# Weights ahead of the second chunk, attention behind the first group, squares shared between two engines

## The chip, the cores and the metric

The kernel runs on one core of a Trainium2 chip. The metric is the device time of one execution in microseconds (us). The core has a matrix engine (PE, with its weight loads shown as PEld), a vector engine (DVE), a scalar engine (ACT), a general engine (POOL), which also issues most of the loads, and SP, which issues the stores and some transposes. Each engine runs its own instructions in the order in which the program writes them and waits on semaphores for the others.

## The reference

Two layers, one behind the other. The first is a decaying linear attention over 4 batches, 8 heads, 768 positions and a head width of 64:

```python
for b in range(nb):                       # 12 blocks of 64 positions
    intra = einsum('bhic,bhjc->bhij', qb, kb) * Dmask      # lam ** (i - j), lower triangle
    intra = einsum('bhij,bhjd->bhid', intra, vb)
    inter = einsum('bhid,bhde->bhie', qb * lam_pow, kv_state)
    out[:, :, sl] = intra + inter
    kv_state = lam_block * kv_state + einsum('bhsd,bhse->bhde', kb * rev_pow, vb)
```

Its output, seen as 3072 rows of 512, goes through a two-layer network with 2048 hidden columns:

```python
h = x @ w_in
s = sin(alpha * h)
g = h + s * s / alpha
return g @ w_out
```

## The kernel before

The 768 positions are cut into six chunks of 128. One chunk of all four batches is a group of 512 rows; the network runs group by group (g = 0 to 5). For a group there are 16 hidden blocks of 128 columns (f = 0 to 15). `hidden(g, f)` issues four PE matmuls into a PSUM bank (L386), a sine on ACT (L389) and, for most f, the square on ACT too (L392). `finish(g, f)` issues on DVE the square, where `squarer` gives it to DVE (L400), and then the sum that writes one block of `gall` and frees the bank (L401). Three banks turn in rotation, so that `hidden(g, f)` needs the bank that `finish(g, f - 3)` frees; in group 0 the first seven blocks have a bank each.

The second matrix product is cut into 16 **units** a group: unit (m, part) is four matmuls (L411), which add four `gall` blocks times a quarter of `w_out` into the bank of 128 output rows m. The fourth part of an m is followed by `store(g, m)`: a copy out of PSUM, on ACT for group 0 and on DVE for groups 1 to 3, and a store issued by SP. Units wait in a list, `behind`; `run(n)` issues the next n of them. For group 0 the list has the parts of m = 0 and 1 in turn, then those of m = 2 and of m = 3.

The attention of chunk t = g + 1 has to be written into `xt[g + 1]` before `hidden(g + 1, 0)` can start. Chunks 0 and 1 are done whole, one batch b at a time: `turns` (eight PE transposes of k and q and one copy to SBUF on ACT, L235), `scores1` (eight matmuls, L256, and two DVE products with the decay mask, L260) and `outs` (four matmuls with the state, L267, eight with v, L271, and one DVE product that writes `xt`, L278). `states1` makes the state after a chunk (L286 on PE, L294 or L297 on DVE, casts on POOL, L301). From chunk 2 on the steps stand in slots of the group's loop: states and `update` (L315, L297), `scores` and `masks` (L334, L341), `outputs` and `leave` (L352, L360, L368), and `turn_by_dma` transposes k and q by DMA. `decay_k` is a POOL product (L204) that the states need.

The program's order is written out by hand. Group 0's loop holds the attention of batch 0 and part of batch 1 of chunk 1 in its last three turns, and four units, at f = 10, 12, 14 and 15. Between group 0 and group 1 stands the **bridge**: the rest of chunk 1's attention with three units between. Group 1's loop calls `run(1)` in every turn but 0, 2, 4, 6, 10 and 12, which takes the nine units that are left. From group 2 on each turn has one unit of the group before.

POOL issues the loads in order: chunk 0, `w_in` in five transfers, `w_out` 0 and 1, `decay_k` of chunk 0 and the six loads of chunk 1 in mixed order, `w_out` 2 and 3, then the loads of chunk 2. Half a chunk is two batches (called "a" and "b" below); each of k, q and v is one transfer a half.

Of the kernel before, what the change touches and what calls it, by code (L numbers as in the profile page):

```python
# [11 lines left out]
BF16 = mybir.dt.bfloat16  # L12
# [3 lines left out]
def kernel(  # L16
# [11 lines left out]
    nc = tc.nc  # L28
# [5 lines left out]
    HP = H // 2  # L34
# [23 lines left out]
    def bank(nm, n, dtype=FP32):  # L58
        return psum.tile([P, 512 if dtype is FP32 else 1024], dtype, name=nm, tag=f"b{n}")
# [28 lines left out]
    def load_w_in(i):  # L88
        nc.gpsimd.dma_start(out=w_in_sb[i][:],
                            in_=moe_w_in[:, i * 512:(i + 1) * 512].rearrange("(c p) g -> p c g", p=P))  # L90

    def load_w_in0(n):
        w = slice(256 * n, 256 * n + 256)
        nc.gpsimd.dma_start(out=w_in_sb[0][:, :, w], in_=moe_w_in[:, w].rearrange("(c p) g -> p c g", p=P))

    def load_w_out(i):
        nc.gpsimd.dma_start(out=w_out_sb[i][:],
                            in_=moe_w_out[i * 512:(i + 1) * 512, :].rearrange("(f p) d -> p f d", p=P))

    def load(t, nm, b0, b1):  # L100
        dst, src = NAT[nm]
        nc.gpsimd.dma_start(  # L102
            out=dst[t][:, b0:b1, :, :].rearrange("p b h e -> p (b h) e"),
            in_=src[b0:b1, :, t * T:(t + 1) * T, :].rearrange("b h p e -> p (b h) e"))
# [13 lines left out]
    iden = consts.tile([P, P], BF16, name="iden")  # L118
# [19 lines left out]
        load(0, nm, b0, b1)  # L138
    load_w_in0(0)
    load_w_in0(1)  # L140
    for i in range(1, 4):
        load_w_in(i)

    lnlam = consts.tile([P, H], FP32, name="lnlam")
    nc.scalar.activation(out=lnlam[:], in_=lam_bc[:], func=ACTF.Ln)
# [40 lines left out]
    V, G, A = nc.vector, nc.gpsimd, nc.scalar  # L186
    xt = {}
    kdec = {}
    KT, QT, both = {}, {}, {}
    STm = {}  # L190
    def home(t, blk):
        return SBD[2 if blk else t % 2]

    def new_xt(t):
        xt[t] = xtp.tile([P, NDC, GRP], BF16, name="xt")
# [4 lines left out]
    def decay_k(t, b0, b1):  # L200
        if t not in kdec:
            kdec[t] = kdp.tile([P, B, H, D], BF16, name="kdec")
        R = later["R128" if t < 2 else "R64"]
        nc.gpsimd.tensor_tensor(out=kdec[t][:, b0:b1, :, :], in0=kn[t][:, b0:b1, :, :],  # L204
                                in1=R[:].unsqueeze(1).unsqueeze(3).broadcast_to([P, b1 - b0, H, D]),
                                op=ALU.mult)

    def new_turned(t):
        QKT = trp.tile([P, 2, B, HP, T], BF16, name="QKT")
        KT[t], QT[t] = QKT[:, 0], QKT[:, 1]  # L210
        both[t] = QKT
# [9 lines left out]
    def turns(t, b, n, engines=None):  # L221
        ps = bank("T_ps", n, BF16)[:].rearrange("p (n c i) -> p n c i", n=2, c=HP)
        if t not in KT:
            new_turned(t)
        for n, src in enumerate((kn, qn)):
            for hp in range(HP):
                nc.tensor.transpose(out=ps[:, n, hp, :], in_=src[t][:, b, 2 * hp:2 * hp + 2, :], identity=iden[:])  # L227
        if engines:
            for n, eng in enumerate(engines):
                if eng is nc.scalar:  # L230
                    eng.copy(out=both[t][:, n, b, :, :], in_=ps[:, n])
                else:
                    eng.tensor_copy(out=both[t][:, n, b, :, :], in_=ps[:, n])
        else:
            nc.scalar.copy(out=both[t][:, :, b, :, :], in_=ps)  # L235

    def halves(hd):
        return slice(hd * D, (hd + 1) * D)

    def turns_pair(t, nm, b, bk, engines):  # L240
        ps = bank("T_ps", bk, BF16)[:].rearrange("p (u c i) -> p u c i", u=2, c=HP)
        src, n = (kn, 0) if nm == "k" else (qn, 1)
        for u in range(2):
            for hp in range(HP):
                nc.tensor.transpose(out=ps[:, u, hp, :], in_=src[t][:, b + u, 2 * hp:2 * hp + 2, :], identity=iden[:])
        for u, eng in enumerate(engines):
            if eng is nc.scalar:
                eng.copy(out=both[t][:, n, b + u, :, :], in_=ps[:, u])  # L248
            else:
                eng.tensor_copy(out=both[t][:, n, b + u, :, :], in_=ps[:, u])  # L250

    def scores1(t, b, ns):
        Fb = [bank("F0_ps", n)[:].rearrange("p (c i) -> p c i", c=HP) for n in ns]
        for hp in range(HP):
            for hd in range(2):
                nc.tensor.matmul(out=Fb[hd][:, hp, :], lhsT=KT[t][halves(hd), b, hp, :],  # L256
                                 rhs=QT[t][halves(hd), b, hp, :], start=True, stop=True)
        st = work.tile([P, 2, HP, T], BF16, name="STm")
        for hd in range(2):
            nc.vector.tensor_tensor(out=st[:, hd], in0=Fb[hd], in1=C0[:, hd], op=ALU.mult)  # L260
        STm[t, b] = st

    def outs(t, b, n, eng=None):
        O = bank("O_ps", n)[:].rearrange("p (c i) -> p c i", c=HP)
        if t:
            for hp in range(HP):
                nc.tensor.matmul(out=O[:, hp, :], lhsT=home(t, 0)[:, b, hp, :, :], rhs=QT[t][:, b, hp, :],  # L267
                                 start=(hp == 0), stop=False, skip_group_check=True)
        for hp in range(HP):
            for hd in range(2):  # L270
                nc.tensor.matmul(out=O[halves(hd), hp, :], lhsT=vn[t][:, b, 2 * hp + hd, :],  # L271
                                 rhs=STm[t, b][:, hd, hp, :], start=(t == 0 and hp == 0), stop=True,
                                 skip_group_check=True)
        x = xt[t][:, :, b * T:(b + 1) * T]
        if eng is nc.scalar:
            nc.scalar.copy(out=x, in_=O)
        else:
            nc.vector.tensor_tensor(out=x, in0=O, in1=Etab[:], op=ALU.mult)  # L278
# [95 lines left out]

    def squarer(g, f):
        if g == 0:
            return V if f in (1, 4, 7, 10, 13) else A
        if g == 1:
            return V if f in (2, 5, 8, 11) else A
        return A  # L380
# [56 lines left out]
    def spin(n, cols=512):  # L437
        ps = bank("hps", HB[0])
        for _ in range(n):
            nc.tensor.matmul(out=ps[:, 0:cols], lhsT=fill[:, 0:P], rhs=fill[:, 0:cols], start=True, stop=True)  # L440
# [20 lines left out]
    nc.tensor.transpose(out=a_ps[:, 0:NFC], in_=alpha_fp[:], identity=idf[:])  # L461
    alpha_sb = consts.tile([P, NFC], FP32, name="alpha_sb")
    r_sb = consts.tile([P, NFC], FP32, name="r_sb")
    turns_pair(0, "k", 2, 1, (A, A))
    spin(6)
    turns_pair(0, "q", 2, 2, (A, V))
    nc.vector.tensor_copy(out=alpha_sb[:], in_=a_ps[:, 0:NFC])
    nc.vector.reciprocal(out=r_sb[:], in_=alpha_sb[:])
    scores1(0, 2, (6, 7))
# [5 lines left out]
    outs(0, 2, 1)  # L475
    outs(0, 3, 2)
    spin(2)
    load_w_out(0)
    load_w_out(1)
    decay_k(0, 0, 2)  # L480
    load(1, "k", 0, 2)
    load(1, "q", 0, 2)
    decay_k(0, 2, 4)
    load(1, "v", 0, 2)
    for nm in "kqv":
        load(1, nm, 2, 4)
    load_w_out(2)
    load_w_out(3)


    new_xt(1)
# [19 lines left out]
    def run(n):  # L511
        for _ in range(min(n, len(behind))):
            behind.pop(0)()

    queue_units(0, [(m, part) for part in range(4) for m in (0, 1)] + [(m, part) for m in (2, 3) for part in range(4)])
    for f in range(NFC):
        hidden(0, f)
        if f in (6, 9):
            states1(0, f // 3 - 2, 4 + 2 * (f == 9))
        if f == 13:  # L520
            turns(1, 0, 6)
        if f == 14:
            scores1(1, 0, (4, 5))
            turns(1, 1, 6)
        if f in (10, 12, 14):
            run(1)
        if f == 15:
            scores1(1, 1, (4, 5))
            outs(1, 0, 6)
            run(1)  # L530
        finish(0, f)
    pair_load(2, 0)
    pair_load(2, 1)
    mask_table()

    outs(1, 1, 1)
    turns(1, 2, 2)
    turns(1, 3, 6)
    run(1)
    scores1(1, 2, (4, 5))  # L540
    run(1)
    scores1(1, 3, (0, 1))
    outs(1, 2, 2)
    outs(1, 3, 6)
    run(1)
    decay_k(1, 0, 2)
    decay_k(1, 2, 4)
    pair_ready(2, 0)
# [35 lines left out]
    for g in range(1, NT + 1):  # L584
        if g < NT:
            gall[g] = gbp.tile([P, NFC, GRP], BF16, name="gall")
        at = slots(g) if g + 1 < NT else {}
        fd = feed(g) if g + 1 < NT else {}
        if g + 1 < NT:
            new_xt(g + 1)  # L590
        for i in range(NFC):
            if g == NT and not behind:
                break
            for a in fd.get(i, []):
                a[0](*a[1:])
            if g < NT:
                hidden(g, i)
            for a in at.get(i, []):
                a[0](*a[1:])
            if g > 1 or i not in (0, 2, 4, 6, 10, 12):  # L600
                run(1)
            if g < NT:
                finish(g, i)
        if g < NT:
            queue_units(g, [(m, part) for m in range(B - 1 if g == NT - 1 else B) for part in range(4)])
# [31 lines left out]
```

## Time and profile before

| what | value |
|---|---|
| median of 3 runs | 215.86 us (215.69 to 217.07) |
| the profiled execution's own time | 215.78 us |
| its span, from first to last instruction | 214.1 us |
| PE busy / DVE busy / ACT busy / POOL busy | 200.0 / 139.0 / 140.6 / 96.4 us |
| group 0's first hidden matmul | 20.40 us |
| group 1's first hidden matmul | 49.67 us |
| end of the attention that group 2 needs | 76.34 us |

The 1.7 us between the span and the time lie around the instructions. PE is busy for 93% of the span, but busy time of PE holds the stretched times of matmuls whose inputs are late, so it is read beside the order of the instructions and not alone. Matmul rows of one merged line follow each other; the distance from one start to the next is the time that a step takes, which is less than the duration of a single record.

### The profile page before, as it was taken

To read this page: it belongs to the slowest core of one execution; us is meant where nothing else is said; L and a number is where in the kernel's file an instruction comes from. 1 tells how busy PE (TensorE), PEld (TensorE's weight loads), DVE (VectorE), ACT (ScalarE), POOL (GpSimd) and SP (SyncE) were. 2 spreads that over 40 slices of the span, in tenths; PEclk is the share of its full clock that TensorE was granted. 3 is DMA by queue.
4 is the path that set the end of the run, shared out by engine and by line. 5 is a ranking of instruction groups with operands and counts; after the bars stand their busy time and mean duration, and the time that the engine had idled before them with its cause. 6 is when DMAs were issued, how large, how long until landed. Compare 5 with 4: busy or idle time off the path is not lost.

```text
span 214.1 us, 4756 instructions
## 1 busy us (share of the span) xinstructions
PE 200.0 (93%) x1913; PEld 100.5 (47%) x1939; DVE 139.0 (65%) x251; ACT 140.6 (66%) x225; POOL 96.4 (45%) x111
## 2 busy tenths in 40 slices
PE   7486989999998999999999999999999999999993
PEld 2354444554444644446444456444446444444453
DVE  7637697865899966995757977648668544444000
ACT  5834997736766497667576765776765778888121
POOL 8999639795699995899001950003100000000000
PEclk9769999999999999999999999999999999999999
DMA  5999999999999999999999114911101001110212
GB/s 113 163 164 206 206 181 156 182 176 158 199 159 161 165 134 129 210 174 115 166 134 163 73 52 104 144 49 52 43 9 49 26 26 49 49 48 5 100 49 98
DMA packets 99782, 24.83 MB, mean 116 GB/s; under 512 B 91936, under 2 KB 96816, under 8 KB 99760
## 3 DMA queue, kind: packets, MB, share of 16 engines
q0 software_dynamic: 75968, 13.24, 84.5%
q1 hardware_dynamic: 23648, 11.28, 26.9%
q8 instruction: 15, 0.25, 0.5%
q14 instruction: 7, 0.06, 0.1%
q10 hardware_dynamic: 144, 0.00, 0.0%
HBM read 27.28 MB, written 6.29 MB: 157 GB/s over the span
## 4 chain that ended last, share of the span: by engine, by line
PE 78%; DVE 10%; ACT 5%; DMA 3%; issue 2%; POOL 1%; POOLq 0%; ACTq 0%
PE ops L411 35%; PE hps L386 32%; DVE gall L401 3%; DMA kn<-in_k_dram 3%; ACT s_sb L389 2%; DVE STm L260 2%; DVE S L297 2%; PE O_ps L352 2%; PE hps L429 2%; ACT s L392 2%; PE O_ps L360 1%; PE T_ps L227 1%; DVE s L400 1%; PE hps L440 1%; PE F_ps L256 1%
## 5 line engine op out<-in xcount | busy, mean ns | idle before, releaser
L401 DVE SCALAR_TENSOR_TENSOR gall<-s,r_sb,hps 128x512 bf16<-128x512 bf16 x96 | 70.9, 744 | 42.3 <-ACT s L392 42.0
L386 PE MATMUL hps<-xt,w_in 128*128 128x512 bf16 x377 | 95.6, 379 | 2.6 <-DVE gall L401 1.5
L389 ACT ACTIVATE s_sb<-hps,alpha_sb 128x512 bf16<-128x512 f32 x96 | 65.6, 687 | 42.7 <-PE hps L386 42.3
L411 PE MATMUL ops<-w_out,gall 128*128 128x512 bf16 x351 | 90.7, 379 | 0.9 <-issue 0.3
L386 PEld LDWEIGHTS <-w_in 128*128 128x128 bf16 x384 | 37.3, 98 | 46.6 <-issue 2.3
L392 ACT ACTIVATE s<-s_sb 128x512 bf16<-128x512 bf16 x87 | 54.9, 632 | 2.8
L411 PEld LDWEIGHTS <-gall 128*128 128x128 bf16 x368 | 34.6, 98 | 40.3 <-issue 0.6
L301 POOL CAST sbd<-S 64x512 bf16<-64x512 f32 x36 | 22.4, 623 | 45.4 <-DVE S L297 43.9
L204 POOL TENSOR_TENSOR kdec<-kn,R 128x1024 bf16<-128x1024 bf16 x12 | 22.6, 1901 | 0.4
L297 DVE SCALAR_TENSOR_TENSOR S<-S,L,KV_ps 128x128 f32<-128x128 f32 x64 | 17.3, 342 | 0.0
L102 POOL DMA_DIRECT2D vn<-in_v_dram x12 | 14.0, 1168 | 1.4 <-DMA w_in<-in_moe_w_in_dram 1.4
L420 ACT COPY o_sb<-ops 128x512 f32<-128x512 f32 x11 | 6.3, 577 | 12.2 <-PE ops L411 12.2
L102 POOL DMA_DIRECT2D kn<-in_k_dram x12 | 14.1, 1173 | 0.5 <-DMA kn<-in_k_dram 0.5
L102 POOL DMA_DIRECT2D qn<-in_q_dram x11 | 13.0, 1180 | 1.7 <-DMA qn<-in_q_dram 1.0
L260 DVE TENSOR_TENSOR STm<-F_ps,C 128x512 bf16<-128x512 f32 x16 | 10.1, 682 | 3.8 <-PE F_ps L256 3.7
L368 DVE TENSOR_TENSOR xt<-O_ps,Etab 128x512 bf16<-128x512 f32 x16 | 10.3, 685 | 2.5 <-PE O_ps L360 2.5
L418 DVE COPY o_sb<-ops 128x512 f32<-128x512 f32 x12 | 8.3, 692 | 4.9 <-PE ops L411 4.9
L341 DVE TENSOR_TENSOR STm<-F_ps,C 128x512 bf16<-128x512 f32 x16 | 10.3, 683 | 0.0
L440 PE MATMUL hps<-fill 128*128 128x512 bf16 x16 | 6.5, 565 | 1.7 <-DVE fill L121 1.5
L235 ACT COPY QKT<-T_ps 128x1024 bf16<-128x1024 bf16 x4 | 3.9, 1008 | 2.2 <-PE T_ps L227 2.2
L256 PE MATMUL F_ps<-QKT 64*128 64x128 bf16 x64 | 3.6, 239 | 1.7 <-ACT QKT L248 0.7
L400 DVE TENSOR_TENSOR s<-s_sb 128x512 bf16<-128x512 bf16 x9 | 5.1, 571 | 0.0
(71 smaller groups left out, 97.6 us busy)
## 6 DMA issues: line engine op xcount, KB each, us to landing
out_dram<-o_sb SPq DMA_DIRECT2D x23, 256.0 KB, 2.3
vn<-in_v_dram POOLq DMA_DIRECT2D x12, 256.0 KB, 15.1
kn<-in_k_dram POOLq DMA_DIRECT2D x11, 256.0 KB, 12.0
qn<-in_q_dram POOLq DMA_DIRECT2D x11, 256.0 KB, 14.0
w_out<-in_moe_w_out_dram POOLq DMA_DIRECT2D x4, 512.0 KB, 15.6
w_in<-in_moe_w_in_dram POOLq DMA_DIRECT2D x3, 512.0 KB, 12.2
raw_q<-in_q_dram SPq DMA_DIRECT2D x2, 256.0 KB, 5.2
w_in<-in_moe_w_in_dram POOLq DMA_DIRECT2D x2, 256.0 KB, 7.3
```

The lines of the kernel that those rows point to most:

```text
L102: nc.gpsimd.dma_start(out=dst[t][:, b0:b1, :, :].rearrange("p b h e -> p (b h) e"), in_=src[b0:b1, :, t * T:(t + 1) * T, :].rearrange("b h ...
L204: nc.gpsimd.tensor_tensor(out=kdec[t][:, b0:b1, :, :], in0=kn[t][:, b0:b1, :, :], in1=R[:].unsqueeze(1).unsqueeze(3).broadcast_to([P, b1 - ...
L260: nc.vector.tensor_tensor(out=st[:, hd], in0=Fb[hd], in1=C0[:, hd], op=ALU.mult)
L297: nc.vector.scalar_tensor_tensor(out=S[:, bs, hp, :], in0=old[:, bs, hp, :], scalar=decay[:, hp:hp + 1], in1=ps[:, :, hp, :], op0=ALU.mult ...
L301: nc.gpsimd.tensor_copy(out=dst[halves(hd), bs, :, hd, :], in_=S[halves(hd), bs, :, :])
L341: nc.vector.tensor_tensor(out=st[:, hd], in0=att["F"][pr, hd], in1=C64[:, hd].unsqueeze(1).broadcast_to([P, 2, HP, D]), op=ALU.mult)
L368: nc.vector.tensor_tensor(out=xview(t)[:, 2 * pr:2 * pr + 2, blk, :, :], in0=att["O"][pr, blk], in1=Eb, op=ALU.mult)
L386: nc.tensor.matmul(out=hps[:], lhsT=w[:, c, (f % 4) * P:(f % 4 + 1) * P], rhs=xt[g][:, c, :], start=(c == 0), stop=(c == NDC - 1))
L389: nc.scalar.activation(out=s_sb[:], in_=hps[:], func=ACTF.Sin, scale=alpha_sb[:, f:f + 1])
L392: nc.scalar.activation(out=s2[:], in_=s_sb[:], func=ACTF.Square)
L401: nc.vector.scalar_tensor_tensor(out=gall[g][:, f, :], in0=s2[:], scalar=r_sb[:, f:f + 1], in1=hps[:], op0=ALU.mult, op1=ALU.add)
L411: nc.tensor.matmul(out=ops[:], lhsT=gall[g][:, f, m * P:(m + 1) * P], rhs=w_out_sb[part][:, f % 4, :], start=(f == 0), stop=(f == NFC - 1))
```

## The change

It moves loads, attention steps, units and squares; no arithmetic is added or taken away.

- Loads: `w_out` 0 goes in ahead of `w_in` 2 and 3; `w_out` 1, 2 and 3 follow, with the two `decay_k` of chunk 0 between, and only then chunk 1.
- Group 0's loop holds no attention of chunk 1 any more. Its four units stand at f = 6, 9, 12 and 14. Seven squares instead of five go to DVE.
- The bridge holds the whole attention of chunk 1, with eight units: three ahead of it and five between its steps. Batches 2 and 3 are turned by `turns_pair`, which now may take two banks and makes four copies instead of two large ones (three on ACT, one on DVE).
- Group 1's loop keeps four units, in turns 2, 5, 8 and 11. With 4 + 8 + 4 there are 16 as before (7 + 9 before).

```diff
     load_w_in0(1)
-    for i in range(1, 4):
-        load_w_in(i)
+    load_w_in(1)
+    load_w_out(0)
+    load_w_in(2)
+    load_w_in(3)
...
     def turns_pair(t, nm, b, bk, engines):
-        ps = bank("T_ps", bk, BF16)[:].rearrange("p (u c i) -> p u c i", u=2, c=HP)
         src, n = (kn, 0) if nm == "k" else (qn, 1)
+        if t not in KT:
+            new_turned(t)
+        one = bank("T_ps", bk[0], BF16)[:].rearrange("p (u c i) -> p u c i", u=2, c=HP)
+        two = one if bk[0] == bk[1] else bank("T_ps", bk[1], BF16)[:].rearrange("p (u c i) -> p u c i", u=2, c=HP)
+        ps = (one[:, 0], two[:, 1])
...
         if g == 0:
-            return V if f in (1, 4, 7, 10, 13) else A
+            return V if f in (1, 3, 5, 8, 10, 12, 14) else A
...
-    load_w_out(0)
     load_w_out(1)
     decay_k(0, 0, 2)
-    load(1, "k", 0, 2)
-    load(1, "q", 0, 2)
+    load_w_out(2)
     decay_k(0, 2, 4)
-    load(1, "v", 0, 2)
-    for nm in "kqv":
-        load(1, nm, 2, 4)
-    load_w_out(2)
     load_w_out(3)
+    for b in (0, 2):
+        for nm in "kqv":
+            load(1, nm, b, b + 2)
...
         hidden(0, f)
         if f in (6, 9):
             states1(0, f // 3 - 2, 4 + 2 * (f == 9))
-        if f == 13:
-            turns(1, 0, 6)
-        if f == 14:
-            scores1(1, 0, (4, 5))
-            turns(1, 1, 6)
-        if f in (10, 12, 14):
-            run(1)
-        if f == 15:
-            scores1(1, 1, (4, 5))
-            outs(1, 0, 6)
+        if f in (6, 9, 12, 14):
             run(1)
         finish(0, f)
...
-    outs(1, 1, 1)
-    turns(1, 2, 2)
-    turns(1, 3, 6)
+    run(3)
+    turns(1, 0, 6)
+    turns(1, 1, 0)
     run(1)
-    scores1(1, 2, (4, 5))
+    scores1(1, 0, (4, 5))
     run(1)
-    scores1(1, 3, (0, 1))
-    outs(1, 2, 2)
-    outs(1, 3, 6)
+    scores1(1, 1, (1, 2))
     run(1)
+    outs(1, 0, 6)
+    turns_pair(1, "k", 2, (0, 0), (A, A))
+    run(1)
+    outs(1, 1, 4)
+    turns_pair(1, "q", 2, (5, 6), (A, V))
+    run(1)
+    scores1(1, 2, (1, 2))
+    scores1(1, 3, (0, 6))
+    outs(1, 2, 4)
+    outs(1, 3, 5)
     decay_k(1, 0, 2)
...
-            if g > 1 or i not in (0, 2, 4, 6, 10, 12):
+            if g > 1 or i in (2, 5, 8, 11):
                 run(1)
```

More of the change, by code (lines that the diff above doesn't have):

```diff
@@ L240, in turns_pair @@
     def turns_pair(t, nm, b, bk, engines):
-        ps = bank("T_ps", bk, BF16)[:].rearrange("p (u c i) -> p u c i", u=2, c=HP)
         src, n = (kn, 0) if nm == "k" else (qn, 1)
+        if t not in KT:
[3 more added lines that the diff above has]
+        ps = (one[:, 0], two[:, 1])
         for u in range(2):
             for hp in range(HP):
-                nc.tensor.transpose(out=ps[:, u, hp, :], in_=src[t][:, b + u, 2 * hp:2 * hp + 2, :], identity=iden[:])
+                nc.tensor.transpose(out=ps[u][:, hp, :], in_=src[t][:, b + u, 2 * hp:2 * hp + 2, :], identity=iden[:])
         for u, eng in enumerate(engines):
             if eng is nc.scalar:
-                eng.copy(out=both[t][:, n, b + u, :, :], in_=ps[:, u])
+                eng.copy(out=both[t][:, n, b + u, :, :], in_=ps[u])
             else:
-                eng.tensor_copy(out=both[t][:, n, b + u, :, :], in_=ps[:, u])
+                eng.tensor_copy(out=both[t][:, n, b + u, :, :], in_=ps[u])
     def scores1(t, b, ns):
@@ L463 @@
     r_sb = consts.tile([P, NFC], FP32, name="r_sb")
-    turns_pair(0, "k", 2, 1, (A, A))
+    turns_pair(0, "k", 2, (1, 1), (A, A))
     spin(6)
-    turns_pair(0, "q", 2, 2, (A, V))
+    turns_pair(0, "q", 2, (2, 2), (A, V))
     nc.vector.tensor_copy(out=alpha_sb[:], in_=a_ps[:, 0:NFC])
```

## The prediction

> **What bounds the kernel now.** I read the page's chain first, then stretches of the span by engine, then DVE and PE in order of time where the change cuts.
>
> ```profile
> PE 78%; DVE 10%; ACT 5%; DMA 3%; issue 2%; POOL 1%; POOLq 0%; ACTq 0%
> PE ops L411 35%; PE hps L386 32%; DVE gall L401 3%; DMA kn<-in_k_dram 3%; ACT s_sb L389 2%; DVE STm L260 2%; DVE S L297 2%; PE O_ps L352 2%; PE hps L429 2%; ACT s L392 2%; PE O_ps L360 1%; PE T_ps L227 1%; DVE s L400 1%; PE hps L440 1%; PE F_ps L256 1%
> ```
>
> The two products of the network carry two thirds of the chain, but DVE has 10% of it, and the times of those pieces lie nearly all before 77 us. So PE sets the end, except early on. The stretches (length, then each engine's busy time) show where:
>
> ```profile
> core 0: us, PE busy (x) PEld busy (x) DVE busy (x) ACT busy (x) POOL busy (x), PEclk, DMA share, GB/s
> 20.40:49.67 29.27, 27.21 (x232) 13.98 (x237) 22.13 (x35) 20.45 (x31) 21.92 (x22) 1.00 1.90 180
> 52.12:76.26 24.14, 23.04 (x328) 12.07 (x331) 23.17 (x50) 16.61 (x27) 20.25 (x22) 1.00 1.99 168
> 76.40:107.40 31.00, 30.79 (x350) 15.33 (x353) 22.99 (x44) 21.95 (x35) 22.17 (x22) 1.00 1.92 154
> ```
>
> First row: from group 0's first hidden matmul to group 1's ("the front"). Second: group 1, from its first DVE sum to the end of `leave`, which lets group 2 start. There DVE is busy 23.17 of 24.14 us: **group 1 is full on DVE as well as on PE**. Third: group 2, dense on PE, DVE with 8 us to spare; the next group looks the same. What is late at 76.4 us therefore stays late to the end, and what is early stays early. The question is when group 2 starts.
>
> **PE work of the front, before.** A step is the distance between starts in the time order. A hidden block or a unit takes 0.862 us (35.21 to 36.07), a batch's transposes 0.44 (two in 43.56 to 44.45), `scores1` 0.33 (46.70 to 47.03), `outs` 0.67 (47.03 to 47.70), `states1` of a pair 0.38 (26.53 to 26.91). 16 hidden blocks 13.79, 7 units 6.03, two `states1` 0.76, four batches of attention 4 x 1.44 = 5.76: 26.3 us of 29.27. So 3.0 us is stall, and that is all the front can give back.
>
> **The change, part by part.** Units move from group 1 (9 to 4) into the front (7 to 12): 5 x 0.862 = 4.31 us of PE work. The work is the same; the gain must come from stalls filled in the front, and the 4.31 us must come back in group 1.
>
> *Group 0's loop* (now without attention). PE: 13.79 + 4 x 0.862 + 0.76 = 18.0, so the last hidden block ends at 20.40 + 18.0 = 38.40. ACT has 16 sines and 9 squares at 0.63: 15.8 from 21.46, ending by 37.3; DVE 16 sums at 0.70, 7 squares at 0.43, two state copies at 0.61: 15.4 from 22.85, ending at 38.3. All three are level, PE sets the pace, and banks are free in time. The two extra DVE squares (+0.86, with 1.26 off ACT) cost nothing under that cover; without it they would cost 0.86. Behind the last block come its sine, square and sum: 38.40 + 0.1 + 0.69 + 0.63 + 0.70 + handoffs = 40.6. Of the three units ahead of the attention two use earlier sums and run to 40.1; the third needs the last sum and waits 0.5, to 41.5.
>
> *The bridge.* From 41.51: transposes of two batches 42.39, unit 43.25, scores 43.58, unit 44.44, scores 44.77, unit 45.63, `outs` 46.30, k transposes 46.74, unit 47.60, `outs` 48.27, q transposes 48.71, unit 49.57, scores of batch 2 49.90. The copies on ACT (0.97 for eight transposes, behind one store copy of 0.57: 43.2 and 44.15) are each done when their scores come up, and the smaller copies of the pairs have 1.7 us of cover. From then on nothing is left to run between: DVE does four products with the mask and two writes of `xt` (0.63 each: four in 45.84 to 48.34), 6 x 0.63 = 3.8 from 50.0, and only then can group 1 start, at **53.9**. Before, the same tail was covered:
>
> ```profile
> 45.73 1.04 PE L411 MATMUL ops<-w_out,gall 128*128 128x512 bf16 x4
> 46.70 0.40 PE L256 MATMUL F_ps<-QKT 64*128 64x128 bf16 x8
> ...
> 48.80 1.04 PE L411 MATMUL ops<-w_out,gall 128*128 128x512 bf16 x3
> 49.67 1.89 PE L386 MATMUL hps<-xt,w_in 128*128 128x512 bf16 x8
> ```
>
> A unit stands between the last two scores and another right before the hidden block; now both pairs of scores come last and no unit follows. So group 1 starts 53.9 - 49.67 = **4.2 us later**: all five units' time, with as much stall as before in another place. It can't be under 3.8: without the 0.5 wait it still is 53.4. The upper end is 5.5, if handoffs of 0.1 between the steps add up.
>
> *Loads.* One issue at a time, POOL's weight transfers land at 20.1, 23.6, 26.1, 28.7 and 31.2, chunk 1 at 33.1, 35.0, 36.8 (k, q, v of a) and 38.6, 40.9, 41.9 (b), `w_out` 2 and 3 at 44.4 and 46.9, chunk 2 from 48.9 on. The queue always holds eight, so I keep its rate and exchange the order: `w_out` 0 lands at 23.6, `w_in` 2 and 3 at 26.1 and 28.7 (needed at 28.6 and 33), the other `w_out` at 31.2, 33.7 and 36.2 (at 34, 38.4 and 40.6), chunk 1 at 38, 40, 41.8 and 43.6, 45.9, 46.9. The uses are k and q of a at 41.5, v of a at 46, k, q and v of b at 46.3, 48.3 and 51: at least 1.5 us of cover each. Three stores of group 0 move to 42 to 50 us; q1's 26.9% of the span for 11.28 MB makes 1.3 us of DMA time each, which can eat that cover but not more than about 2 us beyond. POOL's later work is not late: `decay_k` of chunk 1 can follow the mask table at about 47 and end by 51, used at 55.6. The SP queue holds only the stores and the transposes of group 1, which move with it.
>
> *Group 1.* PE now has 16 hidden blocks, 4 units, two `states1` and 3.5 us of chunk 2's attention: 21.5 us, less than DVE's 23.17. DVE's work is unchanged (16 sums, 4 squares, 24 state updates, 8 products), so DVE is next in line:
>
> ```profile
> 56.68 0.74 DVE L401 SCALAR_TENSOR_TENSOR gall<-s,r_sb,hps 128x512 bf16<-128x512 bf16 x1
> 58.26 0.75 DVE L401 SCALAR_TENSOR_TENSOR gall<-s,r_sb,hps 128x512 bf16<-128x512 bf16 x1 [0.83 <-ACT s L392]
> 58.92 1.44 DVE L400 TENSOR_TENSOR s<-s_sb 128x512 bf16<-128x512 bf16 x1
> 60.40 1.40 DVE L401 SCALAR_TENSOR_TENSOR gall<-s,r_sb,hps 128x512 bf16<-128x512 bf16 x2
> ```
>
> The one gap, 0.83 us, is a wait for ACT, which PE fed late because a unit stood in turn 3; it can go. The square of 1.44 us is the other slack: eight other squares took 0.42 to 0.66. POOL ran `decay_k` beside it:
>
> ```profile
> 58.18 1.90 POOL L204 TENSOR_TENSOR kdec<-kn,R 128x1024 bf16<-128x1024 bf16 x1
> ```
>
> The Trainium skill (SBUF — State Buffer, "Who interferes with whom") says that a DVE instruction with two SBUF inputs and a GpSimd instruction that reads SBUF exclude each other for the whole instruction. This row agrees; by the rule the 1.0 us stays if the two still meet, and goes if not. Both the square and `decay_k` follow the same state updates, so I keep it. Group 1 then gives back between 0 and 0.97 + 1.0 = 2.0 us; I take 0.4, half of the gap that can go, because DVE work behind it waits for other things too.
>
> **Sum.** 4.2 - 0.4 = +3.8 us on the profiled execution's 215.78 (span 214.1 plus 1.7 around): **219.6 us**. The median, 215.86, is the same within 0.1. Ends: 3.8 - 2.0 = +1.8 (217.6) and 5.5 (221.3).
>
> **Rivals.**
> - *Faster: PE alone is the limit.* If the front's stalls are filled down to the work (26.3 + 4.3 = 30.6) and group 1 follows PE's 21.5 plus 0.9 of handoffs, group 2 starts at 20.4 + 30.6 + 22.4 = 73.4, 3 us sooner: 212.8. For it speaks PE's 23.04 of 24.14 in group 1. Against it: DVE would have to do 23.17 us in under 22, and the bridge's tail would have to vanish. It decides where DVE's work in group 1 falls under PE's. 5%.
> - *No change: the five units come back, the tail stays.* Front +4.2, group 1 shorter by all 4.31: 215.7. It needs the same from DVE, after its 2.5 us of start. 12%.
> - *The loads are late.* Chunk 1's second half lands 3 to 4 us later than shifted, by the stores or POOL's issue; less 2 us of cover and the gap of the tail, it adds 1.2 to 2.2: 221.3. Eight transfers in flight speak against it. 13%.
> - *The clock drops.* PE waits some 2.3 us around the two `outs` of the tail, more than any gap of the front before (0.85), where the granted clock stayed 1.00; the first 20 us show 0.83. A stretch of 3.4 us at half clock would add 1.7: 221.3. The Trainium skill (TensorE: Matmul & The Clock Gate, "Why this matters for your kernels") warns of gaps over about 3 us; by that this gap passes. 4%.
>
> **Numbers.** My forecast, +1.8 to +5, has 66%. About 1% (2.2 us) is what a measurement of this kernel tells from no change. A tenth of the forecast lies below that, so slower by over 1% has 0.60 + 0.13 + 0.04 = 0.77, within 1% 0.06 + 0.12 = 0.18, faster 0.05. The range, 217.2 to 221.3, leaves out the first two rivals and a fifth of the last two.
>
> **What would show it.** Group 1's first hidden matmul near 53.9, after DVE's four mask products and two `xt` writes with PE waiting; DVE nearly full from 56.3 to about 80; group 2 from 80.1. Wrong if `leave` of chunk 2 ends before 78, or if PE waits for a transfer in the bridge.

## The result, and the profile after

| | kernel before | changed kernel |
|---|---|---|
| median, first measurement | 215.89 us | 219.42 us (218.27 to 220.1, 4 runs) |
| ratio, 95% interval | | 1.0155 [1.0119, 1.0191] |
| median, second measurement | 215.86 us | 219.52 us (217.99 to 221.85, 6 runs) |
| ratio, 95% interval | | 1.0143 [1.0087, 1.0198] |
| profiled execution, its span | 215.78, 214.1 us | 218.27, 216.5 us |

The change costs 3.5 us by the medians. In the second measurement 8 of 11 executions of the kernel before and 3 of 6 of the changed one have a mean granted clock above 0.98 and take 215.2 to 216.2 and 218.0 to 218.8 us; the others have 0.976 to 0.977 and take 217.1 to 217.6 and 220.3 to 221.9 us. The traces differ in when group 0's first hidden matmul starts: at 19.6 to 19.9 us where the clock from 10 to 16 us is 0.72, at 20.6 to 21.5 us where it is 0.50 to 0.55. So they are compared from that matmul on. The **front** ends with the last write of the group's `xt` (`outs`), **group 1** with the end of `leave`; it is cut in two at the first update of the states.

| us | front | group 1, first half | second half | both stages | rest of the span |
|---|---|---|---|---|---|
| before | 29.22 | 12.10 | 14.62 | 55.94 | 137.76 |
| changed | 33.36 | 11.03 | 14.52 | 58.91 | 137.69 |

Front +4.14, group 1 -1.17, the rest equal to 0.1: **+2.97 us**. The profiled execution of the changed kernel began its first hidden matmul 0.5 us sooner, which hides that much in its span.

The page's chain of the changed kernel, by engine:

```profile
PE 68%; DVE 12%; DMA 8%; POOL 5%; issue 3%; ACT 2%; POOLq 0%; ACTq 0%
```

DVE has more of it than before. (The DMA share has grown from 3% by a transfer for a later chunk that was issued at 102 us, and POOL's by the issues ahead of it; since the rest of the span is the same, they cost nothing.) Three stretches, with length and busy times: the front, group 1 from its first hidden matmul on, and group 2:

```profile
core 0: us, PE busy (x) PEld busy (x) DVE busy (x) ACT busy (x) POOL busy (x), PEclk, DMA share, GB/s
19.90:53.32 33.42, 31.38 (x253) 16.05 (x257) 23.61 (x38) 20.71 (x33) 22.22 (x22) 1.00 1.89 186
53.32:78.87 25.55, 21.97 (x331) 11.25 (x336) 22.22 (x51) 18.08 (x29) 21.04 (x22) 1.00 1.78 151
78.87:109.87 31.00, 30.84 (x350) 15.34 (x353) 22.90 (x44) 20.77 (x33) 23.49 (x23) 1.00 1.80 146
```

In group 1 PE has lost five units of work (25.63 us busy before, 21.97 now), and the stage is only 1.2 us shorter: DVE is busy for 22.22 us of it (23.31 before). In the second half DVE is busy for 14.45 of 14.52 us (14.55 of 14.62 before). The chain in order of time (start, length, what) says the same: from the states' update at 64.29 us on it is DVE alone for 14 us, and PE starts group 2 when `leave` is done:

```profile
67.10 2.07 DVE S L303 x8
...
72.79 1.20 DVE STm L347 x2
...
77.62 1.21 DVE xt L374 x2
78.83 0.04 issue
78.87 1.02 PE hps L392 x4
```

PE in order of time at the end of the bridge:

```profile
48.41 0.81 PE L417 MATMUL ops<-w_out,gall 128*128 128x512 bf16 x3
49.15 0.62 PE L262 MATMUL F_ps<-QKT 64*128 64x128 bf16 x16
49.71 0.40 PE L273 MATMUL O_ps<-QKT,sbd 128*128 128x128 bf16 x4
...
53.32 1.89 PE L392 MATMUL hps<-xt,w_in 128*128 128x512 bf16 x7 [0.81 <-DVE xt L284]
```

Between 49.71 and 53.32 PE has two `outs`, 1.34 us of work in 3.61: 2.3 us go by in the tail, which DVE's four products and two writes fill:

```profile
49.58 2.48 DVE L266 TENSOR_TENSOR STm<-F_ps,C 128x512 bf16<-128x512 f32 x4 [0.71 <-PE F_ps L262]
51.98 1.28 DVE L284 TENSOR_TENSOR xt<-O_ps,Etab 128x512 bf16<-128x512 f32 x2
```

### The profile page after: what moved, and what is told of

The parts are those of the page before. It is cut to its first block, busy times and chain, and to the rows that moved or that the text cites. A ratio compares the mean times of both kernels' runs of the same rounds, so it can differ in the third digit from the quotient of the medians.

```text
span 216.5 us, 4759 instructions
## 1 busy us (share of the span) xinstructions
PE 200.8 (93%) x1913; PEld 100.6 (46%) x1939; DVE 139.3 (64%) x254; ACT 138.9 (64%) x224; POOL 96.4 (45%) x111
## 4 chain that ended last, share of the span: by engine, by line
PE 68%; DVE 12%; DMA 8%; POOL 5%; issue 3%; ACT 2%; POOLq 0%; ACTq 0%
PE ops L417 30%; PE hps L392 29%; DMA qn<-in_q_dram 6%; DVE S L303 3%; DVE gall L407 3%; DMA kn<-in_k_dram 3%; DVE STm L266 2%; PE hps L435 2%; PE T_ps L251 1%; DVE xt L284 1%; DVE xt L374 1%; DVE STm L347 1%; PE hps L446 1%; POOL kn L102 1%; POOL sbd L307 1%
## 5 line engine op out<-in xcount | busy, mean ns | idle before, releaser
L407 DVE SCALAR_TENSOR_TENSOR gall<-s,r_sb,hps 128x512 bf16<-128x512 bf16 x96 | 70.9, 745 | 42.5 <-ACT s L398 42.1
L398 ACT ACTIVATE s<-s_sb 128x512 bf16<-128x512 bf16 x85 | 53.5, 630 | 2.7
L307 POOL CAST sbd<-S 64x512 bf16<-64x512 f32 x36 | 22.3, 620 | 44.0 <-DVE S L303 42.4
L446 PE MATMUL hps<-fill 128*128 128x512 bf16 x16 | 7.2, 617 | 1.7 <-DVE fill L121 1.5
L254 ACT COPY QKT<-T_ps 128x512 bf16<-128x512 bf16 x6 | 3.3, 587 | 6.8 <-PE T_ps L251 6.8
L277 PE MATMUL O_ps<-STm,vn 128*64 128x128 bf16 x64 | 3.8, 223 | 1.9 <-DVE STm L266 1.9
```

What stands on the lines that cost most here:

```text
L307: nc.gpsimd.tensor_copy(out=dst[halves(hd), bs, :, hd, :], in_=S[halves(hd), bs, :, :])
L398: nc.scalar.activation(out=s2[:], in_=s_sb[:], func=ACTF.Square)
L407: nc.vector.scalar_tensor_tensor(out=gall[g][:, f, :], in0=s2[:], scalar=r_sb[:, f:f + 1], in1=hps[:], op0=ALU.mult, op1=ALU.add)
```

## The experiments

All times of stages are from the profiled executions, ratios from the timed runs.

**Units given back to group 1.** Is it the five units that make the front long?

```diff
-        if f in (6, 9, 12, 14):
+        if f in (9, 12):
...
-    run(3)
+    run(1)
...
     turns_pair(1, "q", 2, (5, 6), (A, V))
-    run(1)
...
-            if g > 1 or i in (2, 5, 8, 11):
+            if g > 1 or i not in (0, 2, 4, 6, 10, 12):
```

> The changed kernel with its five moved units given back to group 1 (group 0's loop keeps two units, the bridge five, group 1 nine, as before the change); loads, squares and the attention behind the loop stay. Theory (the front grows by the units only in part; the other part is the attention chain itself, which stands behind the loop and ends in an uncovered tail of DVE work): group 1 starts about 2 us sooner than in the changed kernel, still about 2 us later than before, and group 1 is as long as before; 217.5 us. Rival (the five units are the whole loss): the front falls by all 4.3 us, 215.9 us or less.

Ratio 1.0109 [1.0005, 1.0214], median 218.64. The front is 31.89 us, 1.5 less than in the changed kernel; the halves of group 1 are 12.09 and 14.60, the same as before. So 4.31 us of PE work came out of the front and 1.5 came back. PE got to the transposes at 37.3 us and there waited for chunk 1 (0.41 us for k, 1.49 for q), and the tail stayed (3.60 us, 3.61 in the changed kernel). The rival's number was missed, but this run does not refute it: without these 1.9 us, which the changed kernel does not wait, the front would be about 30.0 us by estimate, the five units giving back up to 3.4. By its interval the time is unclear; the median lies 1 us above the traced execution (217.65 us).

**The loads alone**, on the kernel before: the first and fourth part of the diff, nothing else.

> The kernel before, with the new order of the loads alone. Theory (the new order costs nothing by itself in the changed kernel only because its attention stands later): k and q of chunk 1 land near 38 and 40 us instead of 33 and 35, its transposes stand at 36.1 us in the loop of group 0, so PE waits in the loop and group 1 starts 3 us later: about 219 us. Rival (the loads are hidden anyway): 215.9 us.

Ratio 1.0193 [1.009, 1.0295], median 221.0. PE waits in group 0's loop, as expected:

```profile
39.45 0.40 PE L229 MATMUL T_ps<-iden,qn 128*128 128x128 bf16 x4 [1.35 <-DMA qn<-in_q_dram]
```

The front is 31.69 us, of which 0.83 is a half clock at its start (0.50 from 20 to 22 us; 28 matmuls in 7.03 us, not 6.20). The remaining 1.6 us are the loads' doing, less than the 3 us expected: the transposes came up at 37.72 us instead of 36.07, so k had landed and only q was late. The median lies 2.2 us above the traced execution (218.77 us), which this trace can't explain. In both runs so far in which the attention stands early, the new order of the loads makes PE wait.

**Units given back, and the old order of the loads.** What is left of the change is the place of the attention and group 0's squares.

```diff
-    load_w_in(1)
-    load_w_out(0)
-    load_w_in(2)
-    load_w_in(3)
+    for i in range(1, 4):
+        load_w_in(i)
...
+    load_w_out(0)
     load_w_out(1)
     decay_k(0, 0, 2)
+    load(1, "k", 0, 2)
+    load(1, "q", 0, 2)
+    decay_k(0, 2, 4)
+    load(1, "v", 0, 2)
+    for nm in "kqv":
+        load(1, nm, 2, 4)
     load_w_out(2)
-    decay_k(0, 2, 4)
     load_w_out(3)
-    for b in (0, 2):
-        for nm in "kqv":
-            load(1, nm, b, b + 2)
```

Beside these it has the edits of the first experiment.

> The run with the units given back, with the loads in the order of the kernel before besides: of the change only the place of chunk 1's attention and the squares are left. Theory (with the new order that run lost 1.9 us at the first transposes, to k and q of chunk 1; the old order takes that wait away and puts one for the third quarter of w_out in its place, which lands at 44.4 us and is wanted by the fourth unit of the bridge, near 41 us): the front does not get shorter than 31 us, 217.5 to 218.5 us. Rival (the new order is what made that front long): 30.0 us, about 216.6 us.

Ratio 1.0289 [1.023, 1.0349], median 221.96, the slowest of all. The wait moved to `w_out` and is 4.6 us long, more than expected:

```profile
39.27 0.40 PE L260 MATMUL F_ps<-QKT 64*128 64x128 bf16 x8
44.28 1.41 PE L415 MATMUL ops<-w_out,gall 128*128 128x512 bf16 x4 [4.61 <-DMA w_out<-in_moe_w_out_dram]
```

The front is 36.0 us. Beside the wait it holds a second loss: the granted clock is 0.50 from 45 to 48 us, behind the 4.6 us in which PE stood still, and for this unit, the scores and the next unit PE took 3.56 us, where the first experiment has 2.17. So the place of the attention needs `w_out` early, and early `w_out` needs the attention late: the parts of the change depend on each other, and there the loads do what they are for.

**Units in the tail.** The changed kernel with the same eight units in the bridge, set otherwise (the turns of `outs` and `turns_pair` unchanged):

```diff
-    run(3)
+    run(2)
     turns(1, 0, 6)
     turns(1, 1, 0)
     run(1)
     scores1(1, 0, (4, 5))
     run(1)
     scores1(1, 1, (1, 2))
     run(1)
...
     turns_pair(1, "k", 2, (0, 0), (A, A))
-    run(1)
     outs(1, 1, 4)
     turns_pair(1, "q", 2, (5, 6), (A, V))
-    run(1)
     scores1(1, 2, (1, 2))
     scores1(1, 3, (0, 6))
+    run(1)
     outs(1, 2, 4)
+    run(1)
     outs(1, 3, 5)
+    run(1)
```

> The changed kernel with the same eight units in the bridge, three of which now stand in its tail: one behind the last scores, one between the last two outs, one behind them (two units ahead of the attention instead of three, one each behind the transposes, the first and the second scores). Theory (most of what the front lost is the tail that no unit covers): group 1 starts 2 us sooner after group 0's first hidden matmul, 31.2 instead of 33.4 us; group 1 itself stays near 25.6 us; about 217.2 us. Rival (the front's length is its PE work, and the order in it costs nothing): no change, 219.4 us.

Ratio 1.0076 [1.0047, 1.0104], median 217.15: 2.3 us below the changed kernel. The front is 31.66 us, 1.7 less, group 1 25.58 as expected. The two traced executions, 218.27 and 217.09 us, agree with 1.7 once their starts (19.90 and 20.44 us) are taken off; the other 0.6 us between the medians of two measurements is in no trace. In the tail no wait over 0.16 us is left (ahead of it PE waits 0.53 us for ACT's copy):

```profile
48.46 0.81 PE L417 MATMUL ops<-w_out,gall 128*128 128x512 bf16 x3 [0.16 <-issue]
49.10 0.39 PE L273 MATMUL O_ps<-QKT,sbd 128*128 128x128 bf16 x4
49.42 0.41 PE L277 MATMUL O_ps<-STm,vn 128*64 128x128 bf16 x8
49.77 1.04 PE L417 MATMUL ops<-w_out,gall 128*128 128x512 bf16 x4
...
51.30 1.04 PE L417 MATMUL ops<-w_out,gall 128*128 128x512 bf16 x4
52.18 1.89 PE L392 MATMUL hps<-xt,w_in 128*128 128x512 bf16 x8
```

The same work in another order, and 1.7 us of the 2.3 us of stall are filled: the rival (the order costs nothing) falls.

**Four units left out of group 1**, on the kernel before.

```diff
             def unit(g=g, m=m, part=part):
-                project(g, m, part)
+                if not (g == 0 and m in (2, 3) and part in (1, 2)):
+                    project(g, m, part)
```

> The kernel before, with four of the nine units of group 1 left out (16 matmuls; two quarters of the sums of output rows m = 2 and 3 of group 0 are missing, nothing else). Theory (group 1 is full on DVE as well as on PE, so PE work taken out there is worth little): DVE's 23.2 us of 24.1 stay, the time falls by 0.5 to 1.5 us, to about 214.9. Rival (PE alone sets group 1): all 4 x 0.862 = 3.45 us come back, 212.4 us.

Ratio 1.0009 [0.9958, 1.006]. Halves of 12.08 and 14.60 us against 12.10 and 14.62: 3.45 us of PE work taken out (in turns 5, 7, 11 and 13) gave nothing at all, not even the 0.5 us that I allowed. This is the plainest answer to where the five units' time went: in these turns there was none to gain. The first half keeps its two marks, the wait for ACT behind the unit that still stands in turn 3, and the long square:

```profile
58.70 0.75 DVE L401 SCALAR_TENSOR_TENSOR gall<-s,r_sb,hps 128x512 bf16<-128x512 bf16 x1 [0.83 <-ACT s L392]
59.36 1.43 DVE L400 TENSOR_TENSOR s<-s_sb 128x512 bf16<-128x512 bf16 x1
```

**Squares of group 1 to ACT**, in the changed kernel.

```diff
-            return V if f in (2, 5, 8, 11) else A
+            return A
```

> The changed kernel with the four squares of group 1 that DVE does given to ACT. Theory (group 1 is full on DVE): DVE loses 4 x 0.43 = 1.7 us of work there, ACT with 16 x 1.27 = 20.3 us becomes nearly level, and the end of the second chunk's attention comes 0.5 to 1.7 us sooner: about 218.6 us. Rival (PE or the handoffs set group 1): no change, 219.4 us.

Ratio 1.0123 [1.0078, 1.0168], median 218.8. First half 11.02, as in the changed kernel, second half 13.69 instead of 14.52. The 0.83 us are the two squares of blocks 8 and 11, 0.42 each; the two of the first half gave nothing. So the second half is DVE's work end to end, and the first is not.

**One square of group 1 to ACT**, in the kernel before: that of block 5, the long one of the prediction.

```diff
-            return V if f in (2, 5, 8, 11) else A
+            return V if f in (2, 8, 11) else A
```

> The kernel before, with one square moved: that of block 5 of group 1 goes from DVE to ACT, the one that took 1.43 us beside POOL's product. Theory (DVE sets group 1 in the kernel before as well, and loses 1.0 us in that meeting): from group 1's start to the end of the next attention 25.6 to 26.1 us instead of 26.7; the time 0.6 to 1.1 us lower, about 215.0. Rival (PE with its nine units sets group 1): no change, 215.6 us.

Ratio 0.9992 [0.9973, 1.0012]: no gain. The long square is gone, and DVE waits for ACT in its place (0.83, 0.49 and 0.61 us ahead of three sums, the whole of group 1 26.69 us). With units in turns 1, 3 and 5, PE feeds ACT late. So relieving one of the two did not help in either run: DVE held the first half when PE had less to do, ACT's late squares when DVE had.

**Other turns for group 1's units**, in the kernel before.

```diff
-            if g > 1 or i not in (0, 2, 4, 6, 10, 12):
+            if g > 1 or i in (2, 5, 8, 9, 10, 11, 12, 13, 14):
```

> The kernel before with nothing changed but the turns in which group 1 has its nine units: 2, 5 and 8 to 14 instead of 1, 3, 5, 7, 8, 9, 11, 13, 14. Theory (the first half of group 1, up to the first update of the states, is set by PE and loses about 1 us per unit that stands there; the second half is set by DVE, where PE has 1.7 us to spare): first half 8.5 us from the first sum to the update instead of 9.6, as in the changed kernel, second half 14.6 as before; 1 us less in all, about 214.8 us. Rival (group 1 is one balance, its length does not hang on where the units stand): no change, 215.8 us.

Ratio 1.0044 [1.0007, 1.0082]: not faster. First half 11.02 us, 1.1 less, as in the changed kernel; but the second 15.15, with DVE waiting for PE's `outs` (0.53), and the rest of the span 138.16, 0.4 us more. With units in turns 10 and 12 too, PE is still at work for group 1 when `leave` ends: its first matmul of group 2 comes 0.5 us behind that end (78.64 us), in the kernel before at once. The theory was right on the first half and wrong on the slack of the second.

**Both gains, tail and squares**: the edits of two experiments above, the units in the tail and all of group 1's squares on ACT, in one kernel.

> The version with three units in the tail, and all squares of group 1 on ACT besides. Theory: the two gains add up, the front 31.2 us and group 1 24.7 us, together 55.9 us, the same as in the kernel before (55.9): about 215.7 us. Rival (group 1 is set by PE once it starts sooner): only the front's gain, 217.2 us.

Ratio 1.0038 [1.0008, 1.0069], median 216.45 against 215.81. 219.42 - 216.45 = 3.0 us below the changed kernel, against 2.3 and 0.6 apart: they add up, and the kernel before is still ahead. In its trace group 1 is 24.74 us, as expected, and the front 33.93, of which 2.3 are a half clock at the start (28 matmuls in 8.46 us): 31.7 without it, 0.5 more than expected.

**A mixed version**, meant to beat both; the kernel before with other places for its units.

```diff
-            return V if f in (2, 5, 8, 11) else A
+            return V if f in (2, 8, 11) else A
...
-        if f in (10, 12, 14):
+        if f == 9:
...
-            run(1)
+            run(2)
...
-            if g > 1 or i not in (0, 2, 4, 6, 10, 12):
+            if g > 1 or i not in (0, 1, 4, 5, 12):
```

> A version meant to beat both: the kernel before, with the square of block 5 of group 1 on ACT, and its units set otherwise: in group 0's loop one at f = 9 and two at f = 15, in the bridge three as before, in group 1 ten, in turns 2, 3 and 6 to 11 and 13 to 15 but 12. Theory (PE should not be ahead of DVE in group 0's loop, and not behind it in group 1): the front 0.5 us shorter, group 1 0.5 to 1 us shorter; about 214.5 us. Rival: units in group 1 make PE late again, 215.6 us or more.

Ratio 1.0072 [1.0052, 1.0093]. (The ten units fill turns 2, 3, 6 to 11, 13 and 14.) The front did come out shorter, 28.17 us, and group 1 longer, 28.77: PE stood still for v of chunk 2.

```profile
62.21 0.45 PE L315 MATMUL KV_ps<-vn,kdec 64*64 64x64 bf16 x32 [2.41 <-DMA vn<-in_v_dram]
```

In the kernel before this transfer landed at 57.8 us. There two stores held SP's queue until 54.3; here the first DMA transposes went out at 48.6, as soon as k had landed, and shared the DMA engines with the load, which was issued at 42.07 and landed at about 62. The next run issues them two turns later, has other turns for the units, and the squares of before:

```diff
-            d[2] += [(turn_by_dma, 2, 0)]
+            d[4] += [(turn_by_dma, 2, 0)]
...
-            if g > 1 or i not in (0, 1, 4, 5, 12):
+            if g > 1 or i not in (0, 1, 3, 4, 6, 15):
```

> The mixed version again (group 0's loop with one unit at f = 9 and two at f = 15), with the squares of before, ten units of group 1 in turns 2, 5 and 7 to 14, and the first DMA transposes of chunk 2 issued in turn 4 instead of turn 2, behind two stores in SP's queue as in the kernel before. Theory (in the mixed version PE waited 2.4 us for v of chunk 2, whose transfer shared the DMA engines with transposes that ran 6 us earlier than before): that wait goes, the front stays 28.2 us, group 1 comes to 26 us; 214.2 us. Rival (the load is late for want of time, not because of the transposes): the wait stays, 216 us or more.

The wait for v is gone (what is left ahead of that matmul is 0.49 us for POOL): with the transposes from 57.1 us on, v was issued at 42.43 and landed 14.8 us later, at 57.2. The front is 30.68 us, of which 2.3 are a half clock at its start (28 matmuls in 8.47 us), so 28.4 without it. The first half is 11.02 us, but ten units make the second half 15.82, with DVE waiting for PE's `outs` (0.92); group 1 is 26.84 us, not 26. Ratio 0.9982 [0.9961, 1.0003], 215.53 us against 215.91: unclear, at best 0.2%. No version beat the kernel before clearly.

**The changed kernel again**, unchanged.

> The changed kernel once more, in more rounds beside the kernel before. Theory: the traces differ by 58.9 - 55.9 = 3.0 us between group 0's first hidden matmul and the end of chunk 2's attention and agree in the rest, so the median should lie 3.0 us above the kernel before, near 218.8 us, and what the first measurement had beyond that is the spread of the start. Rival (the change also lengthens the part ahead of 20 us): 3.5 us or more above.

3.66 us above the kernel before, so the rival's number, but not for its reason: group 0's first hidden matmul starts at 19.64 to 21.50 us in the seven traces with the new order of the loads, and at 19.82 to 21.12 us in the seven with the old one. The last section shows the trace.

## Why the prediction was right, point by point

- **The front: +4.2 predicted, +4.14 measured.** Its end was given as 33.5 us after the first hidden matmul and is 33.42. The scores of batch 2 start 29.25 us after it (29.17 predicted); DVE's chain of six takes 3.68 (3.8). The close agreement is in part luck. One term was not there: the third unit was to wait 0.5 us for group 0's last sum, but the three ran dense (38.12 to 40.73). Only the fourth of its matmuls uses that sum, which ended at 40.45 us; by the steps that matmul was due at 40.49. In its place the loop took 0.2 us longer than counted, and the steps from the transposes to the scores of batch 2 took 0.4 us longer (8.42 us instead of 8.06). The floor is a slip: 53.4 - 49.67 is 3.7, not 3.8.
- **The tail as the place of the stall** is shown by the run that put units into it: 1.7 us of its 2.3 came back without any work taken away.
- **Group 1 full on DVE: right for the second half.** 3.45 us of PE work left out gave nothing in either half, and two squares taken from DVE shortened the second half by just their own time. What the prediction lacked is that the halves differ: the first hangs on when PE feeds ACT, and so on the turns in which units stand.
- **The give-back of group 1 was mis-sized:** 0.4 taken, 1.17 measured, inside the 0 to 2.0 given. The failed step is "I keep it" on the meeting of the square with POOL's product. No unit stands in turn 3 now, so DVE did not wait in turn 4, and the square came 0.06 us ahead of POOL's product, not behind it. DVE, then POOL, in the changed kernel:

```profile
60.27 1.51 DVE L407 SCALAR_TENSOR_TENSOR gall<-s,r_sb,hps 128x512 bf16<-128x512 bf16 x2
61.70 0.42 DVE L406 TENSOR_TENSOR s<-s_sb 128x512 bf16<-128x512 bf16 x1
```

```profile
61.76 2.11 POOL L206 TENSOR_TENSOR kdec<-kn,R 128x1024 bf16<-128x1024 bf16 x1
```

  Now it is POOL's product that is long (2.11, not 1.90); in the other order the square took 1.44 us. The order decides it in all ten traces in which the two meet: in four the square starts 0.06 us ahead and takes 0.42, the product 2.11 or 2.12; in six the product starts ahead and takes 1.90, the square 1.43 to 1.70. This agrees with the Trainium skill's rule (SBUF — State Buffer, "Who interferes with whom") that the first to issue holds the port and the other waits. The square's 1.0 us is nearly all of the 1.07 by which the first half came out shorter. The gap of 0.83 us, half of which the 0.4 stood for, only moved: DVE waits 0.72 us for ACT ahead of the sum of block 6 instead.
- **The loads were hidden**, as costed: no wait of PE for a transfer in the bridge. The cover was real but not large: with five units given back to group 1, PE waited 1.9 us in the same place.
- **The sum:** 4.14 - 1.17 = 2.97 us in the first traces, where 3.8 was forecast; the medians say 3.5 and 3.7. That the forecast of the time came nearer than its terms is luck: it had 0.8 us too little give-back, and the medians hold something that it did not count. In one trace this is a lower clock; for the other executions the cause is open.
- **The rivals in which PE alone sets group 1** fell with the run that left units out. The clock rival was priced at 1.7 us, and the one trace that shows it lost 2.05, but by another sum: 0.8 us in the hidden blocks, and most of the rest because the square fell behind POOL's product again. One of the five traces with this tail shows it, so 4% looks too low; the prediction judged it by single gaps (last section).

## What to carry to other kernels

Work moved off an engine that is full buys nothing in a stage where a second engine is just as full; count both before moving it, half by half, and look at what the work was covering where it stood. In a chain of small dependent steps keep the filler for its end: of the 2.3 us that the chain left open with the units ahead of it, units inside it closed 1.7. And an order of loads that is free in one layout can cost 1.6 us and more in the next, because another step has become the first to want them.

## What the runs showed that was not expected

**The clock fell in the tail without a long gap.** In the trace of the second measurement (221.85 us) the front is as long as ever, 33.37 us, but group 1 takes 27.60 instead of 25.55. Its stretches: the tail, the first two hidden blocks, and what follows; the third column from the right is the granted clock.

```profile
51.23:54.84 3.61, 1.88 (x29) 1.30 (x26) 3.56 (x6) 0.14 (x1) 3.61 (x3) 0.95 2.45 161
54.84:57.60 2.76, 2.76 (x7) 1.01 (x7) 0.00 (x0) 0.83 (x2) 0.13 (x1) 0.50 1.88 208
57.60:62.00 4.40, 4.40 (x48) 1.97 (x47) 3.82 (x10) 3.16 (x5) 1.35 (x2) 0.97 1.48 138
```

Eight hidden matmuls took 3.3 us instead of 1.8, the first sum came 0.8 us later, and the square met POOL's product again (1.70 us). These 2.05 us, and a start 1.5 us later (21.41 instead of 19.90), are nearly the whole difference between the two traced executions. In the first trace the same tail, with the same 1.88 us of PE records in 3.61, kept 1.00. PE never waited for longer than 0.81 us at a time there. So the drop came behind a stretch that is half idle in small pieces, in this one trace and not in four others with the same tail (the first, units given back with either order of the loads, and squares of group 1 to ACT). In one piece, PE's wait of 2.41 us in the mixed version left the clock at 1.00, and that of 4.61 us for `w_out` was followed by 0.50. The Trainium skill (TensorE: Matmul & The Clock Gate, "Why this matters for your kernels") puts the limit at idle gaps of about 3 us. The last two agree with it; the drop in the tail came without such a gap. What decides between the five tails was not tried, and whether the clock fell there in executions without a trace is not shown.

**The clock is low at the start of group 0 too, in some traces.** In the trace of the version with other turns it is 0.50 from 20 to 25 us, and 28 hidden matmuls take 8.45 us, not 6.20; two more traces (both gains, and the second mixed version) show the same. What decides it was not tried.

**DMA transposes that start while a load is in flight go with a later landing of it:** v of chunk 2, issued at 42.1 to 42.4 us in all three, landed at 57.8 in the kernel before, at about 62 with the transposes from 48.6 us on, and at 57.2 with them from 57.1 us on. The changed kernel's two traces and that with units in the tail point the same way: the transposes start 4.3, 6.0 and 7.5 us behind v's issue, and v lands 17.6, 16.7 and 15.0 us behind it. Stores that are in flight in the same time were not separated from them.
